# Respacing the weight-sum steps, giving the last weights' narrowing a buffer of its own, and turning block 0's rows inside the last expert tile

## The chip, the cores and the metric

The kernel runs on one core of a Trainium2 chip. What counts is the device time of one launch in microseconds (us), as the median of several runs. Five engines work side by side, each through a queue of its own that it takes in order: TensorE (PE, matmuls), VectorE (DVE), ScalarE (ACT), GpSimd (POOL) and SyncE (SP, which only issues transfers). ACT and POOL issue transfers too, in line with their other work.

## What is computed

Three stages over 4608 rows of 512 numbers:

```python
x = attention(q, k, v)                      # chunks of 64, 8 heads
# mixture of experts: rows with x @ w_skip > 0 go to the best of 8 experts
h = np.maximum(xc[mask] @ w1[e], 0.0)       # 512 -> 1024
y[mask] = gate_w[mask, None] * (h @ w2[e])  # 1024 -> 512
out[do_compute] = xc + y
# last stage, over all rows ("moe2")
h = np.maximum(np.maximum(x @ w1, x @ w2), x @ w3)   # 512 -> 768
return (h @ w_out).astype(np.float32)                # 768 -> 512
```

The four weight matrices of the last stage come in 64-bit floats and are narrowed to 32 bits on the chip.

## The kernel before

Every product is made of three matmuls: each operand is split into a high part that TensorE takes exactly and the rest, and high*high, low*high and high*low are added (`mm3`, L705 to L707). The high part is an ACT cast (L90, L517, L575, L884), the low part a subtraction on DVE or POOL (L91, L518, L576, L885).

Attention takes the first 213 us. Then the experts run one after the other, e = 0 to 7. `first_tiles` makes h for the expert's first row tiles in four pieces, called h_0, h_2, h_4 and h_6 here (hhi on ACT L711, hlo on DVE L712), and then y by `second`; after y, DVE adds it to the rows (xg<-y, L694) and POOL scatters them to x_dram (L696). A third tile (`single`) and more of them stand behind branches on the expert's row count (L983, L916, L920). When such a branch is not taken, all engines meet there, and TensorE goes on with the next expert only after DVE has passed the branch too. In this input experts 1, 4 and 6 end at the first such branch; expert 0's always runs its third tile, and experts 2, 3 and 5 take the branch.

The last stage turns x by a 2x2 block scheme with seven products in place of eight. Its weights therefore have to be narrowed, added up and split in advance: 18 steps, two for each of nine units (matrix m = 0 to 2, column block f = 0 to 2). A step is `sums_ahead(i)`: load n_raw, narrow it into n_q (DVE L531, L532, L533, L536 and an ACT square L534), four sums on DVE (L569 to L572), the ACT cast L575, the DVE remainder L576, and two stores to m2_sums: the high part from the ACT queue (L577), the low part from SP, or for i >= 11 from POOL (L578). Steps 0 to 10 run among the experts: the table STEPS says how many in each, and `first_tiles` puts one behind a piece of h. In the experts n_q is one buffer, so a step's first instruction waits for the store of the step before it. Steps 11 to 17 run in block 0 of the last stage, one in each of units 0 to 6; there n_raw has three buffers (shared with raw_m, below) and n_q two, of the tag "s4".

The last stage goes over five blocks of rows. For a block `sums_T` turns the rows (PE trf L879, tr11, tr12, tr21, tr22), makes the sums t1 to t4 (DVE L893 to L900) and splits everything. Each of the nine `unit`s then makes seven products into three accumulators a, b and d. An accumulator is used again after another engine has read it: ACT copies the first a (p1), the first d (p5) and the second a (u2), DVE adds the third a to p5 (L1034) before the fourth goes into the same place. The weights of a product (ws) come back from m2_sums by SP loads through a ring (L851). At the end of a block come the products with w_out (o). The six halves of w_out are narrowed by `m2_direct` in block 0: load raw_m (POOL queue, L812), narrow into n_q_m, split into whi_m and wlo_m. A scheduler writes the order of each engine's queue; the program gives it dependencies and a few lower bounds (`issue_after`).

In the names of the traced rows the numbers are left out: n_q stands for n_q0 to n_q17, f_a for the accumulator a of any unit.

## Time and profile before

| | us |
|---|---|
| median of 3 runs | 1106.93 (1106.44 to 1108.24) |
| the profiled execution | 1109.83, span 1108.1 |
| PE busy | 1042.2 (94%) |
| DVE busy | 614.8 (55%) |
| ACT busy | 446.2 (40%) |
| POOL busy | 309.1 (28%) |

The profile is of one execution. PE is busy nearly all of it; the granted clock of TensorE is at its full level but for short stretches at half. What a change can give is therefore in the places where PE waits, and in the stretches at half clock. A row of a timeline gives the start and the length of an instruction, its engine, its line and what it writes and reads, and in brackets how long the engine had idled before it and what ended that.

### The profile page before, as it was taken

To read this page: it belongs to the slowest core of one execution; us is meant where nothing else is said; L and a number is where in the kernel's file an instruction comes from. 1 tells how busy PE (TensorE), PEld (TensorE's weight loads), DVE (VectorE), ACT (ScalarE), POOL (GpSimd) and SP (SyncE) were. 2 spreads that over 40 slices of the span, in tenths; PEclk is the share of its full clock that TensorE was granted. 3 is DMA by queue.
4 is the path that set the end of the run, shared out by engine and by line. 5 is a ranking of instruction groups with operands and counts; after the bars stand their busy time and mean duration, and the time that the engine had idled before them with its cause. 6 is when DMAs were issued, how large, how long until landed. Compare 5 with 4: busy or idle time off the path is not lost.

```text
span 1108.1 us, 17499 instructions
## 1 busy us (share of the span) xinstructions
PE 1042.2 (94%) x6320; PEld 872.1 (79%) x6320; DVE 614.8 (55%) x1299; ACT 446.2 (40%) x774; POOL 309.1 (28%) x297
## 2 busy tenths in 40 slices
PE   7899799988899998998899799999999999999997
PEld 6788677777788787887687588878888888788996
DVE  6687588756756477671499772335244442443241
ACT  6677487434434244431444342222322232223231
POOL 4124232364404044320432160222312140123021
PEclk9999799999899999999999999999999999999999
DMA  9999996257764468544898934663566545666591
GB/s 211 195 216 232 261 229 183 89 195 259 265 217 136 138 211 273 192 150 141 274 319 285 300 114 136 197 190 114 165 194 192 166 139 166 183 186 208 186 288 38
DMA packets 217513, 216.99 MB, mean 196 GB/s; under 512 B 50219, under 2 KB 179403, under 8 KB 217408
## 3 DMA queue, kind: packets, MB, share of 16 engines
q1 hardware_dynamic: 206384, 183.62, 57.3%
q0 software_dynamic: 8432, 23.76, 6.6%
q10 hardware_dynamic: 2592, 8.26, 1.9%
q8 instruction: 60, 0.98, 0.4%
q14 instruction: 45, 0.37, 0.1%
HBM read 175.15 MB, written 41.83 MB: 196 GB/s over the span
## 4 chain that ended last, share of the span: by engine, by line
PE 41%; DMA 6%; DVE 3%; issue 3%; POOL 1%; ACT 0%; SPq 0%; POOLq 0%; DVEq 0%; ACTq 0%
PE f_a L705 5%; PE f_a L707 5%; PE f_a L706 5%; PE o L705 4%; PE o L707 4%; PE o L706 4%; DMA ws<-m_sums 3%; PE f_d L705 3%; PE f_d L707 3%; PE f_d L706 3%; DMA m_sums<-n_q 2%; PE f_b L705 1%; PE f_b L707 1%; PE f_b L706 1%; PE trf L879 1%
## 5 line engine op out<-in xcount | busy, mean ns | idle before, releaser
L91 POOL TENSOR_TENSOR fh<-best,fh 128x512 fp32r<-128x512 f32 (+1 forms) x60 | 77.0, 1290 | 356.3 <-ACT fh L90 270.4
L705 PE MATMUL f_a<-x_t,ws 128*128 128x512 f32 (+1 forms) x270 | 100.7, 373 | 5.0 <-DVE p L1034 4.8
L706 PE MATMUL f_a<-x_t,ws 128*128 128x512 f32 (+1 forms) x270 | 99.9, 370 | 0.0
L707 PE MATMUL f_a<-x_t,ws 128*128 128x512 f32 (+1 forms) x270 | 99.7, 370 | 0.0
L90 ACT CAST whi_e<-raw_e 128x1024 fp32r<-128x1024 f32 x64 | 65.1, 1045 | 60.0 <-DMA raw_e<-in_moe_w_dram 34.8
L705 PE MATMUL h<-xhi,whi_e 128*128 128x256 f32 x256 | 75.5, 295 | 12.2 <-DVEq L983 7.0
L706 PE MATMUL o<-wlo_m,fh 128*128 128x512 f32 x216 | 84.6, 392 | 0.0
L705 PE MATMUL o<-whi_m,fh 128*128 128x512 f32 x216 | 83.4, 392 | 0.0
L707 PE MATMUL o<-whi_m,fh 128*128 128x512 f32 x216 | 83.4, 392 | 0.0
L91 DVE TENSOR_TENSOR wlo_e<-raw_e,whi_e 128x1024 fp32r<-128x1024 f32 x50 | 67.1, 1351 | 18.1 <-ACT whi_e L90 15.9
L705 PE MATMUL y<-whi_e,hhi 128*128 128x512 f32 x184 | 74.3, 406 | 2.6 <-ACT hhi L772 1.8
L707 PE MATMUL y<-whi_e,hlo 128*128 128x512 f32 x184 | 72.8, 400 | 1.8 <-DVE hlo L712 1.6
L706 PE MATMUL h<-xlo,whi_e 128*128 128x256 f32 x256 | 74.4, 291 | 0.0
L707 PE MATMUL h<-xhi,wlo_e 128*128 128x256 f32 x256 | 74.3, 290 | 0.0
L706 PE MATMUL y<-wlo_e,hhi 128*128 128x512 f32 x184 | 72.3, 395 | 0.0
L696 POOL DMA_INDIRECT x_dram<-xg,ids_sb x20 | 20.6, 1030 | 180.2 <-DVE xg L694 72.8
L90 ACT CAST fh<-best 128x512 fp32r<-128x512 f32 (+1 forms) x60 | 34.7, 579 | 89.5 <-DVE best L1036 57.9
L1039 ACT COPY p<-f_a 128x512 f32<-128x512 f32 (+1 forms) x45 | 24.5, 545 | 99.3 <-PE f_a L707 99.1
L705 PEld LDWEIGHTS h<-xhi,whi_e 128*128 128x128 f32 x256 | 51.0, 199 | 15.3 <-ACTq L983 6.3
L705 PEld LDWEIGHTS f_a<-x_t,ws 128*128 128x128 f32 x270 | 51.2, 190 | 14.5 <-DVE p L1034 5.3
L707 PEld LDWEIGHTS f_a<-x_t,ws 128*128 128x128 f32 x270 | 51.2, 190 | 8.6
L706 PEld LDWEIGHTS f_a<-x_t,ws 128*128 128x128 f32 x270 | 51.2, 190 | 8.3
(226 smaller groups left out, 2678.7 us busy)
## 6 DMA issues: line engine op xcount, KB each, us to landing
ws<-m_sums SPq DMA_DIRECT2D x135, 512.0 KB, 5.2
raw_e<-in_moe_w_dram SPq DMA_DIRECT2D x64, 512.0 KB, 5.1
ws<-m_sums SPq DMA_DIRECT2D x45, 256.0 KB, 3.9
v_bd<-in_v_dram SPq DMA_DIRECT2D x144, 64.0 KB, 4.2
x<-x_dram SPq DMA_DIRECT2D x36, 256.0 KB, 4.9
out_dram<-os SPq DMA_DIRECT2D x36, 256.0 KB, 2.0
x_dram<-xg SPq DMA_DIRECT2D x17, 512.0 KB, 4.2
m_sums<-n_raw ACTq DMA_DIRECT2D x18, 448.0 KB, 6.0
```

What stands on the lines that cost most here:

```text
L90: nc.scalar.copy(hi, src),
L91: eng.tensor_tensor(lo, src, hi.bitcast(F32), op=ALU.subtract),
L696: ins = nc.gpsimd.indirect_dma_start(out=x_dram[:, :], out_offset=bass.IndirectOffsetOnAxis(ap=ids, axis=0), in_=xg, in_offset=None, bound ...
L705: nc.tensor.matmul(acc, ahi, bhi, start=first, stop=False, skip_group_check=onto)
L706: nc.tensor.matmul(acc, ahi, blo, start=False, stop=False, skip_group_check=onto)
L707: return nc.tensor.matmul(acc, alo, bhi, start=False, stop=last, skip_group_check=onto)
L879: nc.tensor.transpose(tr[:, i * P:(i + 1) * P], row[:, c * P:(c + 1) * P], ident)
L1039: nc.scalar.copy(p1, acc_a)
```

## The change

Four edits. (1) STEPS gives expert 0 one step in place of two and expert 5 two in place of one, and the second step of an expert is put behind the piece h_4 in place of h_2. (2) `m2_direct` narrows into a buffer of its own (n_q_m, one of them) in place of the two "s4" buffers that it shared with the steps. (3) The six pieces of w_out come one after unit 3, one after unit 6, two after units 7 and 8; before it was two after each of units 6, 7 and 8. (4) In `sums_T` the split of tr22 comes before the two sums that read it, and block 0's first `sums_T` is issued after the third of eight kf steps of the last expert tile's y, in place of ahead of that y.

```diff
-    def second(name, key, hhi, hlo, i, xg, ids, tag=None):
+    def second(name, key, hhi, hlo, i, xg, ids, tag=None, inside=None):
...
-                mm3(acc, hhi[:, kf, sl], hlo[:, kf, sl], bhi[:, kf % 2, :], blo[:, kf % 2, :], n == 0, n == 7)
+                done = mm3(acc, hhi[:, kf, sl], hlo[:, kf, sl], bhi[:, kf % 2, :], blo[:, kf % 2, :], n == 0, n == 7)
+            if inside and n == 2:
+                with tc.issue_after(done.ins):
+                    inside()
...
-            if n % 2 == 2 - per and side:
+            if n in (0, 4) and side:
...
-    STEPS = [2, 2, 2, 2, 2, 1, 0, 0]
+    STEPS = [1, 2, 2, 2, 2, 2, 0, 0]
...
-        quarters = four_kb([P, 8, P], F32, f"n_q_m{m}_{f}_{half}", True)
+        quarters = fpool.tile([P, 8, P], F32, tag="n_q_m", name=f"n_q_m{m}_{f}_{half}", bufs=1)
...
         tr22 = turned(cc + 2, 1)
+        split_x("b22", tr22, nc.vector)
         nc.vector.tensor_tensor(t2, tr22, t1, op=ALU.subtract)
         nc.vector.tensor_tensor(t3, tr22, b12, op=ALU.subtract)
-        split_x("b22", tr22, nc.vector)
...
-                single(f"{e}_2", (e, 2), *third, lambda: sums_T(0, 0))
+                single(f"{e}_2", (e, 2), *third, inside=lambda: sums_T(0, 0))
...
+        SPREAD = [0, 0, 0, 1, 0, 0, 1, 2, 2]
...
-                if b == 0 and 3 * f + m >= 6:
-                    for _ in range(min(2, len(rest))):
-                        rest.pop(0)()
+                for _ in range(SPREAD[3 * f + m] if b == 0 else 0):
+                    rest.pop(0)()
```

The number of instructions on each engine stays the same. Their order does not, and three places follow. Lines behind the edits stand three or four lower (L694 stays, L983 becomes L986, L1034 becomes L1037).

The first place is DVE at the end of expert 1. n_q1 and n_q2 are the buffers of its two steps, y_1_0 and y_1_1 its two row tiles. Before:

```order
L576 TENSOR_TENSOR n_q1_3965<-n_q1_3965,n_raw1_3963 128x896
L712 SCALAR_TENSOR_TENSOR hlo_1_4542<-h_1_4_4629,hhi_1_4541 128x512
L91 TENSOR_TENSOR wlo_e2_3_4532<-raw_e2_3_4529,whi_e2_3_4531 128x1024
L712 SCALAR_TENSOR_TENSOR hlo_1_4542<-h_1_6_4656,hhi_1_4541 128x512
...
L531 TENSOR_SCALAR n_q2_4572<-n_raw2_4570 128x512
...
L694 SCALAR_TENSOR_TENSOR xg_1_3854<-y_1_0_4714,xg_1_3854 128x512
...
L576 TENSOR_TENSOR n_q2_4572<-n_q2_4572,n_raw2_4570 128x896
L694 SCALAR_TENSOR_TENSOR xg_1_3854<-y_1_1_4743,xg_1_3854 128x512
L973 TENSOR_LOAD cnt_i_130 x2
L983 COMPARE_AND_BRANCH
```

Now:

```order
L91 TENSOR_TENSOR wlo_e2_3_4516<-raw_e2_3_4513,whi_e2_3_4515 128x1024
L712 SCALAR_TENSOR_TENSOR hlo_1_4526<-h_1_6_4640,hhi_1_4525 128x512
L576 TENSOR_TENSOR n_q1_4556<-n_q1_4556,n_raw1_4554 128x896
...
L531 TENSOR_SCALAR n_q2_4626<-n_raw2_4624 128x512
L532 SCALAR_TENSOR_TENSOR n_q2_4626<-n_raw2_4624,n_q2_4626 128x512
L694 SCALAR_TENSOR_TENSOR xg_1_3854<-y_1_0_4698,xg_1_3854 128x512
...
L694 SCALAR_TENSOR_TENSOR xg_1_3854<-y_1_1_4727,xg_1_3854 128x512
L576 TENSOR_TENSOR n_q2_4626<-n_q2_4626,n_raw2_4624 128x896
L976 TENSOR_LOAD cnt_i_130 x2
L986 COMPARE_AND_BRANCH
```

The first step's end (L576 of n_q1, and with it its store) moved behind the piece h_6; the second step's first instruction stayed where it was, ahead of both xg<-y and of the branch.

The second place is ACT in block 0, around unit (m=1, f=1). f_0_2_1_a is accumulator a of the next unit in block 0, p1_0_2_1 its copy; n_q_m3_0_0 is the first half of w_out. Before:

```order
L534 ACTIVATE n_q15_8745<-n_raw15_8664 128x512
L1054 COPY best_0_0_1_2_8655<-f_0_0_1_a_8647 128x512
L575 CAST n_raw14_8566<-n_q14_8666 128x896
L577 DMA m2_sums_1_2_167<-n_raw14_8566 128x896
L1039 COPY p1_0_2_1_8815<-f_0_2_1_a_8812 128x512
L1043 COPY p5_0_2_1_8817<-f_0_2_1_d_8814 128x512
```

Now:

```order
L575 CAST n_raw14_8566<-n_q14_8666 128x896
L534 ACTIVATE n_q_m3_0_0_8726<-raw_m3_0_0_8724 128x512
L1057 COPY best_0_0_1_2_8655<-f_0_0_1_a_8647 128x512
L577 DMA m2_sums_1_2_167<-n_raw14_8566 128x896
L534 ACTIVATE n_q16_8839<-n_raw16_8755 128x512
L90 CAST whi_m3_0_8722<-n_q_m3_0_0_8726 128x512
L575 CAST n_raw15_8664<-n_q15_8757 128x896
L577 DMA m2_sums_1_2_167<-n_raw15_8664 128x896
L575 CAST n_raw16_8755<-n_q16_8839 128x896
L1042 COPY p1_0_2_1_8827<-f_0_2_1_a_8824 128x512
```

The square of n_q_m3_0_0 now stands ahead of the store of step 14, and the square and the cast of step 16 ahead of the copy p1 of unit (2, 1). On POOL the loads of the same stretch were, before:

```order
L547 DMA n_raw15_8664<-in_moe2_w2_dram 128x2x512
L578 DMA m2_sums_0_2_166<-n_q13_8568 128x896
L91 TENSOR_TENSOR fh_0_0_0_8636<-best_0_0_0_2_8396,fh_0_0_0_8636 128x512
L547 DMA n_raw16_8743<-in_moe2_w3_dram 128x2x512
L578 DMA m2_sums_1_2_167<-n_q14_8666 128x896
L547 DMA n_raw17_8825<-in_moe2_w3_dram 128x2x512
```

Now:

```order
L547 DMA n_raw15_8664<-in_moe2_w2_dram 128x2x512
L91 TENSOR_TENSOR fh_0_0_0_8636<-best_0_0_0_2_8396,fh_0_0_0_8636 128x512
L578 DMA m2_sums_0_2_166<-n_q13_8568 128x896
L815 DMA raw_m3_0_0_8724<-in_moe2_w_out_dram 128x1024
L578 DMA m2_sums_1_2_167<-n_q14_8666 128x896
L547 DMA n_raw16_8755<-in_moe2_w3_dram 128x2x512
```

The load of raw_m3_0_0 took the place of the load of n_raw16, which went into the place of n_raw17's; the two after step 13 and after step 14 each wait for that step's high store, which frees their buffer.

The third place is DVE in the same unit; u2_0_1_1 and p5_0_1_1 are read out of accumulators d and a of unit (1, 1). Before:

```order
L1034 TENSOR_TENSOR u2_0_1_1_8734<-u2_0_1_1_8734,f_0_1_1_d_8732 128x512
L572 TENSOR_TENSOR n_q14_8666<-n_q14_8666 128x128
L531 TENSOR_SCALAR n_q15_8745<-n_raw15_8664 128x512
L1036 TENSOR_TENSOR best_0_0_1_1_8654<-best_0_0_1_1_8654,u2_0_1_1_8734 128x512
L532 SCALAR_TENSOR_TENSOR n_q15_8745<-n_raw15_8664,n_q15_8745 128x512
L1034 TENSOR_TENSOR p5_0_1_1_8735<-p5_0_1_1_8735,f_0_1_1_a_8730 128x512
```

Now:

```order
L1037 TENSOR_TENSOR u2_0_1_1_8746<-u2_0_1_1_8746,f_0_1_1_d_8744 128x512
L532 SCALAR_TENSOR_TENSOR n_q15_8757<-n_raw15_8664,n_q15_8757 128x512
L531 TENSOR_SCALAR n_q_m3_0_0_8726<-raw_m3_0_0_8724 128x512
L1039 TENSOR_TENSOR best_0_0_1_1_8654<-best_0_0_1_1_8654,u2_0_1_1_8746 128x512
L576 TENSOR_TENSOR n_q14_8666<-n_q14_8666,n_raw14_8566 128x896
L533 SCALAR_TENSOR_TENSOR n_q15_8757<-n_raw15_8664,n_q15_8757 128x512
L532 SCALAR_TENSOR_TENSOR n_q_m3_0_0_8726<-raw_m3_0_0_8724,n_q_m3_0_0_8726 128x512
L1037 TENSOR_TENSOR p5_0_1_1_8747<-p5_0_1_1_8747,f_0_1_1_a_8742 128x512
```

Between the two reads stand six rows where four stood, and the first instruction on raw_m3_0_0 is among them. On PE the fourth product into f_0_1_1_a now follows the third at once; before, four other products lay between.

## Rows read from the trace of the kernel before

**Rows 1.** What PE waited for: engine, line, releaser; us in total, times, longest.

```profile
PE h L705 <- DVEq L983: 7.0, 3, 3.8
PE f_a L705 <- DVE p L1034: 4.8, 1, 4.8
PE f_a L705 <- DMA ws<-m_sums: 2.3, 2, 1.8
```

**Rows 2.** Busy time by stretch: bounds, length, engines (instructions), granted clock, DMA share, GB/s.

```profile
261.30:274.56 13.26, 13.26 (x98) 13.26 (x99) 13.01 (x16) 8.40 (x10) 9.03 (x5) 0.87 0.75 254
290.59:305.00 14.41, 14.41 (x98) 14.41 (x99) 11.98 (x12) 7.96 (x10) 9.79 (x6) 0.79 0.83 275
343.94:355.69 11.75, 11.75 (x98) 11.75 (x99) 10.22 (x16) 8.32 (x11) 7.78 (x7) 1.00 0.71 231
519.78:530.09 10.31, 8.92 (x39) 7.16 (x38) 2.06 (x3) 1.48 (x3) 0.00 (x0) 0.83 1.07 343
554.00:609.40 55.40, 54.88 (x244) 44.92 (x243) 51.66 (x93) 23.92 (x38) 15.52 (x18) 1.00 0.91 302
609.40:637.10 27.70, 21.06 (x86) 16.23 (x85) 21.82 (x36) 10.20 (x18) 5.46 (x8) 0.94 0.90 300
```

**Rows 3.** Timeline at the ends of experts 0 and 1.

```profile
260.15 0.43 DVE L531 TENSOR_SCALAR n_q<-n_raw 128x512 int32<-128x512 int32 x1 [5.35 <-DMA m_sums<-n_q]
261.30 0.39 PE L705 MATMUL h<-xhi,whi_e 128*128 128x256 f32 x1 [2.81 <-ACTq L916]
274.41 0.46 SPq L578 DMA_DIRECT2D m_sums<-n_q  x1
277.98 0.68 DVE L712 SCALAR_TENSOR_TENSOR hlo<-h,hhi 128x512 fp32r<-128x512 f32 x1
283.19 0.43 DVE L531 TENSOR_SCALAR n_q<-n_raw 128x512 int32<-128x512 int32 x1 [1.61 <-DMA m_sums<-n_q]
290.59 0.55 PE L705 MATMUL h<-xhi,whi_e 128*128 128x256 f32 x1 [3.78 <-DVEq L983]
```

**Rows 4.** Timeline from the end of expert 4 into expert 5.

```profile
408.52 1.75 SPq L97 DMA_DIRECT2D raw_e<-in_moe_w_dram  x3
420.27 0.36 PE L705 MATMUL h<-xhi,whi_e 128*128 128x256 f32 x1 [1.73 <-DVEq L983]
426.34 0.43 DVE L531 TENSOR_SCALAR n_q<-n_raw 128x512 int32<-128x512 int32 x1 [6.28 <-DMA m_sums<-n_q]
438.78 0.50 PE L707 MATMUL y<-whi_e,hlo 128*128 128x512 f32 x1 [1.64 <-DVE hlo L712]
```

**Rows 5.** Timeline, PE's waits at the start of block 0.

```profile
521.90 0.41 PE L879 MATMUL trf<-ident,x 128*128 128x128 f32 x1 [1.39 <-DMA x<-x_dram]
534.35 0.41 PE L879 MATMUL trf<-ident,x 128*128 128x128 f32 x2 [2.16 <-DVE x_b L885]
546.13 0.33 PE L879 MATMUL trf<-ident,x 128*128 128x128 f32 x1 [1.16 <-DMA x<-x_dram]
```

**Rows 6.** Timeline in block 0, units (1, 1) and (2, 1): POOL, ACT and DVE.

```profile
584.65 0.73 POOL L547 DMA_DIRECT2D n_raw<-in_moe_w_dram  x1 [2.73 <-DMA m_sums<-n_raw]
585.52 0.68 DVE L1034 TENSOR_TENSOR u<-u,f_d 128x512 f32<-128x512 f32 x1
587.07 0.94 ACT L575 CAST n_raw<-n_q 128x896 fp32r<-128x896 f32 x1
587.86 0.68 DVE L1034 TENSOR_TENSOR p<-p,f_a 128x512 f32<-128x512 f32 x1
588.04 0.33 ACTq L577 DMA_DIRECT2D m_sums<-n_raw  x1
595.84 0.71 POOL L547 DMA_DIRECT2D n_raw<-in_moe_w_dram  x1 [5.42 <-DMA m_sums<-n_raw]
```

**Rows 7.** DMA issues between 560 and 620 us: count, KB each, median us to landing.

```profile
n_raw<-in_moe_w_dram POOLq DMA_DIRECT2D x4, 512.0 KB, 5.5
raw_m<-in_moe_w_out_dram POOLq DMA_DIRECT2D x4, 512.0 KB, 4.7
```

More of the change, by code (lines that the diff above doesn't have):

```diff
@@ L750, in first_tiles, with single @@
         return hhi, hlo
-    def single(name, key, xT, xg, ids, between=None):
+    def single(name, key, xT, xg, ids, between=None, inside=None):
         e = key[0]
@@ L774, in single @@
         nxt = between() if between else None
-        second(name, key, hhi, hlo, 0, xg, ids)
+        second(name, key, hhi, hlo, 0, xg, ids, inside=inside)
         return nxt
@@ L1059 @@
         rest = [lambda i=i, half=half: m2_direct(3, i, wpool2, half) for i in range(NS) for half in range(2)]
+        SPREAD = [0, 0, 0, 1, 0, 0, 1, 2, 2]
     else:
         rest = [lambda i=i: m2_piece(3, i, wpool2) for i in range(NS)]
+        SPREAD = [0, 0, 0, 0, 0, 0, 1, 1, 1]
     steps = list(range(AHEAD, 2 * len(UNITS)))
```

## The prediction

> **What bounds the kernel now.** I read the page first: PE is busy 94% of the span, so only PE's waits and its stretches at half clock can be won or lost. The list of PE's waits [rows 1] names three sorts that the change touches: the branches at the ends of experts (7.0 us in three waits), one wait of 4.8 for a DVE read of an accumulator, and two for the weights ws. The table by stretch [rows 2] then shows what a wait does to the clock. The 98 matmuls of an expert's h take 11.75 us at full clock; behind the waits at the ends of experts 0 and 1 they take 13.26 and 14.41, with a granted clock of 0.87 and 0.79, that is, with part of the stretch at 1.2 GHz instead of 2.4. In block 0 the row from 554 to 609 us is the important one: PE has next to no gap, 0.227 us per matmul (55.40 over 244), 1.36 us per product of six, 9.5 us per unit, but DVE is busy 51.66 of 55.40. It has some 0.6 us to spare in each unit. The next row (609 to 637) is where PE loses: 21.06 busy of 27.70. Last come the timelines around each wait [rows 3 to 6] and the landing times [rows 7].
>
> **The change, part by part.** Times are on the clock of the profiled execution.
>
> End of expert 0. DVE's L531 of a second step stood 5.35 us for the last store, and xg<-y and the branch behind it; PE waited 2.81 [rows 3]. That step is gone there. What is late next is the branch itself: at the end of expert 4, where DVE is on time, PE waits 1.73 [rows 4], and at full clock afterwards. So 1.1 of the wait and 13.26 - 11.75 = 1.5 of clock: -2.6 (bounds -3 and -1).
>
> End of expert 1. The second step's L531 has kept its place ahead of both xg<-y and the branch, but the store it waits for has moved back: L576 of the first step now stands behind hlo of h_6, which ended at 278.66, and ends an estimated 1.1 later (0.68 for 512 columns, 896 here), at 279.8, where it was issued at 274.41 [rows 3]. That store needed 8.8 us (274.41 to 283.19), since it stood behind loads; the quickest transfers of this size in the rows take 4.7, the usual 5.5 [rows 7]. So L531 starts between 284.5 and 288.6, and I take 5.5: 285.3, 2.1 later than before. From L531 to PE's first matmul it was 7.4 us of the same instructions: PE starts 2.1 later. +2.1 (bounds -1, as L531 idled 1.61, and +5.4); the clock stays as bad as it was.
>
> End of expert 4. This one had no step in its way. Now a whole second step stands between wlo_e and the branch, xg<-y inside it, and its L531 waits for the first step's store, which SP issues only behind the raw_e loads from 408.52 to 410.27 [rows 4]. At 5.5 to 8.8 us it lands between 415.8 and 419.1; 7.4 later PE would start at 423.2 to 426.5, against 420.27. If the store is early, only the cast and L576 behind the last xg<-y are left, about 1. I take +3.5, toward the 8.8 because the store stands behind loads in both places, and 1.5 of clock, as after the 2.81: +5.0 (bounds +0.5 and +7.7).
>
> Expert 5. Its first L531 was the first thing on DVE and idled 6.28 with all wlo_e and hlo behind it, and PE waited 1.64 for a late hlo [rows 4]. It now stands behind hlo of h_0, so the idle time is covered by those: -1.6, and 1.5 of clock, -3.1 (bounds -3.5 and 0). The step that moves into expert 5 meets a branch that is taken, where PE doesn't wait: 0.
>
> Start of block 0. Nine matmuls of y (0.25 each, 2.2 us) now stand ahead of the first transposes, which waited 1.39 for x [rows 5]; the stretch ran at 0.83 [rows 2], so 3.5 of its 10.31 us at half clock, 1.7 lost. Both go. The 2.16 for x_b shrinks to about 0.5: the bank's last reader is one DVE instruction (0.68) earlier, and six matmuls (1.4) stand ahead of the transpose. The 1.16 for block 1's rows goes, since 30 matmuls were put ahead. -1.4 - 1.7 - 1.7 - 1.2 = -6.0; I take -5.5 for a wait on the sums' casts that may take their place (bounds -7 and -3).
>
> Units of block 0. What is removed: 4.8 and 2.3 of waits [rows 1] and 0.06 of 27.70 for the clock [rows 2], 1.7: 8.8. What is put there hangs on three transfers in a row. The load of raw_m_0_0 takes n_raw16's place, 584.65 [rows 6]; it waits for step 13's store as that did. It lands 4.7 later [rows 7], 589.3. Its L531 on DVE comes two instructions after the read of u, at 586.7, and waits 2.6. Behind it stand L1039, L576, L533, L532 and the read p5 of accumulator a: by 0.68 (0.43 for L531, 1.1 for L576), with the ends overlapped by 0.08, 4.0 us; p5 ends at 593.3. PE's fourth product into that accumulator used to have four products of cover; now it follows the third at once, and the third was done by 587.86, when DVE read it. PE waits 5.5.
>
> On ACT the store of step 14 stands behind the square of that same raw_m and a copy: 590.6 instead of 588.04. n_raw16's load waits for it. In the rows this took 7.8 (588.04 to 595.84); with the 5.5 of rows 7 in mind I take 6.3: 596.9. The load takes 5.5: 602.4. DVE goes from there to the last sum of step 16 in 5.4 (seven of 0.6, L576, four sums at 0.2), ACT casts for 0.94, and only then comes the copy p1 that PE's second product in unit (2, 1) needs: 609.4. PE has four products until there, 593.3 + 5.4 = 598.7. It waits 10.7. A third wait, in place of the 4.8, is a bare read of an accumulator with nothing between: 1.2. With 1.5 of clock behind the long one: 5.5 + 10.7 + 1.2 + 1.5 = 18.9, less 8.8: +10. Bounds: if no transfer is late, the first wait is 2.9, the second 0, and it is 4.1 - 8.8 = -4.7; if all three take 7.8, 8.6 + 14.6 + 2.7 - 8.8 = +17.
>
> The Trainium skill ("DMA: Bandwidth & Descriptors", section "Anatomy of one DMA — SWDGE (gpsimd) path") gives a transfer as 2.0 us and its bytes at 436 GB/s, an estimate of 3.2 us for 512 KB. By that the chain would be short: the units come to about +2 and both expert ends to about 0, a total of -9. Rows 7 have 4.7 and 5.5 for these loads with other traffic beside them, so I don't go by it. The same page ("Issuing engines are not separate DMA queues") has transfers of all issuing engines share the same 16 engines; with a DMA share of 0.91 in rows 2 that speaks against bringing a piece of w_out forward, and would add the 1.7 us that 512 KB take at that row's 302 GB/s.
>
> End of block 0. Four groups of transposes follow each other where o matmuls lay between; casts of 0.6 to 0.7 separate their banks: +0.5 (0 to 2). The one buffer of n_q_m makes the narrowings serial; each is some 3 us on DVE and the o products that need the last come over 7 us after unit 8: 0.
>
> Sum: -2.6 + 2.1 + 5.0 - 3.1 - 5.5 + 10 + 0.5 = +6.4. The profiled execution is 1109.83, span 1108.1 and 1.7 around it; it lies 2.9 above the median, and I carry the difference over: 1113.3.
>
> **The rivals.** First, the other side: DVE and ACT reach the moved rows after their data have landed. Then all old waits go and little comes: -2.6, -1.0, +0.5, -3.1, -5.5, -4.7, +0.5, -15.9 in all, 1091. For it: the waits named in rows 1 all lie where the edits are. Against it: in rows 6 a load that stands behind a store was issued 7.8 after it. It decides at landing times: with transfers at 3.2 the total is the -9 above, 1098. These two: 0.24.
>
> Second, the long wait is halved, because step 14 and raw_m come some 5 us sooner against PE, and expert 4's end costs 1: units +5, -2.6 + 2.1 + 1 - 3.1 - 5.5 + 5 + 0.5 = -2.6, 1104 to 1108. Rows 2 give DVE 3.7 us of slack over 5.8 units, which could carry half of that. 0.20.
>
> Third, all of it late at 7.8: the units +17, experts 1 and 4 +5.4 and +7.7, 19.4 in all, 1126. Rows 7 have most transfers quicker. 0.06.
>
> **How the numbers follow.** The forecast, 1113, has 0.50, and 1107 to 1120 as its own range. Runs of the kernel before lie within 1.8 us of each other, so 0.2% (2.2 us) is about what can be told from no change. Faster by more: the first rival, and the lower half of the second, 0.33. Within: 0.15, the rest of the second and the edge of the forecast. Slower: 0.52. For 8 in 10 the range goes from 1095 to 1121.
>
> **What would show it.** In the profile after: PE's wait at the end of expert 0 at 1.5 to 1.8 with h at 11.75; at the ends of experts 1 and 4 waits of 5 to 6 for DVE's branch; no wait for x at the start of block 0. In block 0 the copy p1 behind the casts L575 as PE's longest wait, 10 us, one of 5 for DVE's p in the unit ahead of it, and POOL's n_raw load idle for m_sums<-n_raw. I am wrong if DVE and ACT don't idle at raw_m and n_raw16, and if PE's waits between 585 and 637 come to less than 9 us.

## The result, and the profile after

The kernel after takes 1120.6 us (median of 4 runs, 1119.13 to 1125.96) against 1106.68 for the kernel before (4 runs). The ratio is 1.0133, 95% interval 1.0098 to 1.0169. It is slower, as forecast, and by 13.9 us where 6.4 were forecast: the sign was right, and so were most places, but the forecast was less than half of what came. A second comparison (e11 below) gave 1.0119 (1.0071 to 1.0168). The profiled execution of the kernel after took 1120.28, span 1118.6; that of the kernel before was 1109.83.

The list of PE's waits in the kernel after, from 230 to 670 us (engine, line, what was waited for; us in total, times, longest), against [rows 1]:

```profile
PE h L705 <- ACTq L986: 14.9, 2, 8.6
PE f_a L705 <- DVE p L1037: 7.5, 2, 6.7
PE f_a L705 <- ACT p L1042: 6.1, 1, 6.1
PE h L705 <- DVEq L986: 1.8, 1, 1.8
PE f_a L705 <- DMA ws<-m_sums: 0.9, 1, 0.9
```

The waits at the first branch of an expert (L983 before, L986 now) have gone from 3.8 at most to 8.6 and 6.3. In block 0 there are now two long waits, 6.7 for DVE's p and 6.1 for ACT's p, where one of 4.8 stood. The waits for x at the start of block 0 are not in the list any more.

Busy time by stretch of the kernel after (bounds, length, then PE, PEld, DVE, ACT and POOL with their instructions, granted clock, DMA share, GB/s), against [rows 2]:

```profile
259.48:271.20 11.72, 11.72 (x98) 11.72 (x99) 10.94 (x9) 7.70 (x10) 9.48 (x5) 1.00 0.88 272
289.75:303.20 13.45, 13.45 (x96) 13.45 (x97) 10.23 (x9) 8.12 (x10) 9.00 (x6) 0.84 0.84 300
426.20:440.20 14.00, 14.00 (x101) 14.00 (x102) 11.71 (x11) 8.32 (x11) 9.82 (x6) 0.85 0.94 313
579.79:636.99 57.20, 43.49 (x167) 34.22 (x166) 43.69 (x77) 19.53 (x32) 12.78 (x18) 0.85 0.78 260
587.50:597.80 10.30, 5.68 (x13) 4.46 (x14) 7.57 (x15) 1.70 (x3) 1.99 (x3) 0.50 0.79 258
604.60:611.40 6.80, 4.81 (x11) 3.80 (x12) 2.83 (x5) 3.02 (x5) 1.75 (x3) 0.50 0.93 309
```

Behind expert 0 the h of the next expert now runs at full clock (98 matmuls in 11.72, 13.26 before). Behind the ends of experts 1 and 4 it runs at 0.84 and 0.85. In block 0 PE is busy 43.49 of 57.20, and two pieces of it are at half clock: 5.68 and 4.81 us of matmuls at 1.2 GHz, which would take about half of that at 2.4, so by estimate 5.2 us are lost to the clock there.

How long the stages last, in two profiled executions of each kernel (before and e1; after and e11, all below). A stage ends where the next expert's first matmul of h starts, or at the matmul named, counted among those into the accumulators of the units (378 of them are block 0's). The row of expert 0 starts 15.0 us after that expert's first matmul of h, in all four alike, and the last row ends with PE's last matmul:

| stage | before | e1 | after | e11 | change of the means | forecast |
|---|---|---|---|---|---|---|
| expert 0 | 33.10 | 30.30 | 30.43 | 32.36 | -0.3 | -1.1 |
| expert 1 | 29.29 | 27.01 | 30.27 | 29.59 | +1.8 | +0.6 |
| expert 2 | 53.35 | 50.83 | 52.56 | 52.16 | +0.3 | 0 |
| expert 3 | 50.16 | 50.21 | 51.29 | 52.05 | +1.5 | 0 |
| expert 4 | 26.18 | 27.29 | 32.60 | 32.17 | +5.7 | +3.5 |
| expert 5 | 42.46 | 39.37 | 39.71 | 39.74 | -1.2 | -1.6 |
| expert 6 | 25.44 | 25.38 | 25.77 | 25.81 | +0.4 | 0 |
| expert 7 to the 181st matmul | 93.29 | 90.96 | 88.11 | 88.50 | -3.8 | -5.5 |
| 181st to 391st matmul | 92.14 | 94.38 | 103.52 | 104.21 | +10.6 | +10.5 |
| the rest | 427.94 | 429.43 | 428.72 | 430.25 | +0.8 | 0 |
| sum | 873.35 | 865.16 | 882.98 | 886.85 | +15.7 | +6.4 |

The forecast's terms are put where they act: the slow clock behind a wait belongs to the stage after it. Attention comes ahead of these stages and is not in the table. It took 213 to 216 us in some of the profiled executions and 221 to 228 in others, the kernel before and the kernel after among both, so times are compared within one table row or one ratio only.

### The profile page after: what moved, and what is told of

Its sections match the earlier page's. It is cut to its first block, busy times and chain, and to the rows that moved or that the text cites. A ratio compares the mean times of both kernels' runs of the same rounds, so it can differ in the third digit from the quotient of the medians.

```text
span 1118.6 us, 17488 instructions
## 1 busy us (share of the span) xinstructions
PE 1044.0 (93%) x6320; PEld 873.2 (78%) x6320; DVE 609.2 (54%) x1299; ACT 447.5 (40%) x774; POOL 313.1 (28%) x297
## 4 chain that ended last, share of the span: by engine, by line
PE 44%; DMA 6%; issue 1%; DVE 1%; ACT 1%; POOL 1%; SPq 0%; ACTq 0%; POOLq 0%; DVEq 0%
PE f_a L705 6%; PE f_a L706 6%; PE f_a L707 6%; PE o L705 4%; PE o L706 4%; PE o L707 4%; DMA ws<-m_sums 4%; PE f_d L705 3%; PE f_d L706 3%; PE f_d L707 3%; PE f_b L706 1%; PE f_b L707 1%; PE f_b L705 1%; PE trf L882 1%; DMA m_sums<-n_raw 1%
## 5 line engine op out<-in xcount | busy, mean ns | idle before, releaser
L705 PE MATMUL f_a<-x_t,ws 128*128 128x512 f32 (+1 forms) x270 | 101.4, 376 | 13.6 <-DVE p L1037 7.5
L705 PE MATMUL h<-xhi,whi_e 128*128 128x256 f32 x256 | 75.5, 295 | 19.6 <-ACTq L986 14.9
L696 POOL DMA_INDIRECT x_dram<-xg,ids_sb x20 | 23.2, 1162 | 182.5 <-DVE xg L694 92.2
L1042 ACT COPY p<-f_a 128x512 f32<-128x512 f32 (+1 forms) x45 | 24.4, 544 | 91.3 <-PE f_a L707 91.0
```

The lines of the kernel that those rows point to most:

```text
L696: ins = nc.gpsimd.indirect_dma_start(out=x_dram[:, :], out_offset=bass.IndirectOffsetOnAxis(ap=ids, axis=0), in_=xg, in_offset=None, bound ...
L705: nc.tensor.matmul(acc, ahi, bhi, start=first, stop=False, skip_group_check=onto)
L1042: nc.scalar.copy(p1, acc_a)
```

## The experiments

**e1, the kernel before once more.** No edit.

> The kernel before, unchanged, profiled once more. Theory A (the 2.9 us by which its profiled execution lay above its median belong to that one execution): the new profiled execution lies at 1105.5 to 1108.5, and one or two stretches account for the difference. Rival B (a profiled execution is longer than others by about 3 us whatever the kernel): it lies at 1109 to 1111 again. The kernel after speaks against B already, since its profiled execution (1120.28) lies at its median (1120.6).

Ratio 0.9991 (0.9963 to 1.0020), so two equal kernels compare equal to about 0.3% here. The profiled execution lay at 1109.47, the lowest of ten (median 1117.37). That is in the range that B named, but by luck: B has a profiled execution longer than the others, and this one was shorter, so B falls. A's level was missed too, since all runs of that comparison were some 10 us longer. Its second half holds: the wait at the end of expert 0 was 1.51 where it was 2.81 in [rows 3], and expert 5's wait for a late hlo [rows 4] was not there at all; the two stages were 2.8 and 3.1 shorter, and expert 1 by 2.3.

**e2, edit 4 alone.**

```diff
...
         tr22 = turned(cc + 2, 1)
+        split_x("b22", tr22, nc.vector)
         nc.vector.tensor_tensor(t2, tr22, t1, op=ALU.subtract)
         nc.vector.tensor_tensor(t3, tr22, b12, op=ALU.subtract)
-        split_x("b22", tr22, nc.vector)
...
-                single(f"{e}_2", (e, 2), *third, lambda: sums_T(0, 0))
+                single(f"{e}_2", (e, 2), *third, inside=lambda: sums_T(0, 0))
```

> The kernel before with edit 4 alone (split of tr22 ahead of the two sums, block 0's first transposes inside the last y). Theory A (each edit pays at its own place): -5 to -6 at the start of block 0 and nothing in the experts, 1101 to 1102; the waits in units 5 to 8 of block 0 (7 us before) stay within 2. Rival B (the scheduler lays the units out anew once the start moves, so that the loss of units 4 to 6 is partly edit 4's): a new wait of 3 us or more between 575 and 615 us, and 1104 or more.

Ratio 0.9951 (0.9914 to 0.9988): -5.5 us, as A has it. Expert 7 to the 181st matmul took 86.11, against 93.29, 90.96, 89.96 (e4) and 90.84 (e5) in the kernels that have neither edit 4 nor the new STEPS. PE's waits in e2 from 500 to 675 us:

```profile
PE f_a L705 <- DVE p L1037: 5.1, 1, 5.1
PE h L705 <- DVEq L992: 1.6, 1, 1.6
PE f_b L705 <- DMA ws<-m_sums: 0.8, 1, 0.8
```

The waits for x and x_b of [rows 5] are gone, and nothing new stands between 575 and 615. One part of A is wrong: the wait of 5 for DVE's p in unit 7 stayed (4.8 before, 5.1 here).

**e3, edit 1 alone; e5, only the place of the second step; e6, only the table.**

```diff
# e5 has this line alone, e6 the table alone, e3 both
-            if n % 2 == 2 - per and side:
+            if n in (0, 4) and side:
...
-    STEPS = [2, 2, 2, 2, 2, 1, 0, 0]
+    STEPS = [1, 2, 2, 2, 2, 2, 0, 0]
```

> The kernel before with edit 1 alone (STEPS and the place of the second step). Theory A: -2 at the end of expert 0, +6 at the end of expert 4 with a wait of 8 to 9 us at the branch, -3 in expert 5, together +1 to +3: 1108 to 1110. Rival B (the wait of 8.63 at the end of expert 4 was a slow store of that execution): a wait of 5 us there, as forecast, and -2 to 0 in all: 1105 to 1107.

> The kernel before with the second step of an expert behind h_4 in place of h_2, and STEPS as it was. Theory A (the place makes the loss of edit 1: the second step's narrowing starts a store's time too late for an expert that ends at its first branch): waits of 5 us or more for the branch at the ends of experts 1 and 4, each with slow clock behind it; +6 to +9 us, a ratio of 1.005 to 1.008. Rival B (the table makes it, through the step that came into expert 5): waits of 4 us or less at both, ratio 0.998 to 1.002.

> The kernel before with the new STEPS and the second step behind h_2 as it was. Theory A: end of expert 4 as in the kernel before (wait 1.7 to 2.7), expert 5 no longer than in the other kernels, since its branch is taken: ratio 0.997 to 1.000. Rival B: the second step in expert 5 costs 2 us or more there or at expert 6: ratio 1.003 or more.

e3: 1.0073 (1.0037 to 1.0109), 8.2 us, more than either theory gave it; the long wait at the end of expert 4 that A named is there (8.35). e5: 0.9983 (0.9956 to 1.0010), nothing. e6: 1.0075 (1.0040 to 1.0111). So A was wrong in e5 and in e6: the place costs nothing and the table costs all. B of e6 has the ratio but not the place: expert 5 took 39.81 and expert 6 25.82, as in the stage table, and the loss stands at the end of expert 4. PE's first matmul behind the end of expert 4, in e5 and then in e6 (start, length, engine, line, in brackets the wait):

```profile
432.47 0.36 PE L705 MATMUL h<-xhi,whi_e 128*128 128x256 f32 x1 [1.80 <-DVEq L983]
```

```profile
436.20 0.58 PE L705 MATMUL h<-xhi,whi_e 128*128 128x256 f32 x1 [8.62 <-ACTq L983]
```

The order of DVE's queue says why. The steps are a chain through the one buffer n_q: none can start before the store of the last has landed. With two steps in expert 0, step 6 starts ahead of expert 3's branch (369.20 in the kernel before), step 7 in expert 4's h (404.31), and step 8 behind expert 4's branch (426.34). With one step in expert 0 steps 5 to 7 come 14 to 25 us later, counted from the first matmul of h: step 6 starts with expert 4's h (395.38 in the kernel after), step 7 between the last hlo and the branch (419.10). The place h_4 or h_2 is only a lower bound, and in e5 it moved none of the three to another side of a branch.

**e4, edits 2 and 3 alone.**

```diff
-        quarters = four_kb([P, 8, P], F32, f"n_q_m{m}_{f}_{half}", True)
+        quarters = fpool.tile([P, 8, P], F32, tag="n_q_m", name=f"n_q_m{m}_{f}_{half}", bufs=1)
...
+        SPREAD = [0, 0, 0, 1, 0, 0, 1, 2, 2]
...
```

> The kernel before with edits 2 and 3 alone (own buffer for n_q_m, pieces of w_out after units 3, 6, 7, 8). Theory A (the first piece in unit 3 makes the loss): waits of 5 us or more for DVE's p in unit (1, 1) and for ACT's copy p1 of unit (2, 1), 13 us or more of waits and slow clock beyond the 8.8 that go, +8 to +12: 1115 to 1119. Rival B (the loss needs the order that all four edits make together): less than +4, up to 1111, without the wait for the copy p1.

Ratio 1.0045 (1.0012 to 1.0079), 5.0 us: between the two. PE's waits in e4 from 580 to 690 us:

```profile
PE f_a L705 <- DVE p L1034: 6.8, 1, 6.8
PE f_a L705 <- ACT p L1039: 2.5, 1, 2.5
PE f_a L705 <- DMA ws<-m_sums: 1.7, 1, 1.7
```

Both waits of A are there, the second at 2.5 where the kernel after has 6.1. In e4's order ACT's cast and store of step 14 stand ahead of the square of step 15, which waited 2.96 for the low store of step 13; in the kernel after they stand behind it. Counted from the 181st matmul (583.02 in e4, 579.79 in the kernel after) the store was issued at 3.1 against 8.4, and step 16, whose n_raw waits for it, began on DVE at 16.2 against 19.6. From the 181st to the 391st matmul e4 took 99.89, 6.7 more than the mean 93.2 of six executions without the own buffer and with two pieces after each of units 6, 7 and 8 (before, e1, e2, e3, e5, e6; 91.7 to 95.3, and e9, which is also of this kind, 91.2); the kernel after took 103.9.

The ratios of e2, e3 and e4 multiply to 1.0069, 7.7 us, where all four edits together cost 13.9 and, in e11, 13.3. So by their middle values the edits cost more together than one by one, though the intervals are wide enough to hide it. Of the difference 4.0 can be placed: the units took 103.9 with all edits and 99.89 in e4, with the second wait at 6.1 in place of 2.5. The rest is not placed.

**e7, the kernel after without the piece in unit 3.**

```diff
-        SPREAD = [0, 0, 0, 1, 0, 0, 1, 2, 2]
+        SPREAD = [0, 0, 0, 0, 0, 0, 2, 2, 2]
```

> The kernel after with SPREAD = [0, 0, 0, 0, 0, 0, 2, 2, 2]: own buffer for n_q_m, but no piece of w_out after unit 3. Theory A (that piece makes the loss of the units): no wait of PE above 3 us between 575 and 615 us, the stretch from unit 3 to block 1 as in the kernel before or up to 3 longer (11.4 longer in the kernel after); edit 1's +6 to +8 and edit 4's -5 remain: ratio 1.000 to 1.004. Rival B (one buffer for n_q_m makes the loss, wherever the pieces stand): waits for DVE's p or for ws behind unit 6 take it over, 6 us or more longer than before: ratio 1.007 or more.

Ratio 1.0056 (1.0020 to 1.0093). PE's waits in e7 from 595 to 695 us:

```profile
PE f_a L705 <- DVE p L1037: 2.5, 1, 2.5
PE f_a L705 <- DMA ws<-m_sums: 2.5, 1, 2.5
PE trf L882 <- DVE t L900: 1.0, 1, 1.0
```

No wait above 3, and none of the two long ones: A, though the ratio lies between the two theories. The 181st to the 391st matmul took 95.9, 2.7 more than the mean of 93.2: A's "up to 3". So of the 10.7 by which the kernel after is above that mean, some 8 are the piece after unit 3. The other 2.7 go with the own buffer, but one execution stands against six that spread from 91.7 to 95.3, so that size is rough. The piece after unit 3 in the shared buffers was not run.

**e12, edits 4 and 2, the pieces as before.** e2 with the own buffer of e4.

> The kernel before with edits 4 and 2 (own buffer for n_q_m), the pieces two after each of units 6, 7 and 8 as before. Theory A (the own buffer by itself takes away the wait for step 17's store): 4.8 us and 1.7 of slow clock go in unit 7, against which the one buffer adds no more than 3: ratio 0.990 to 0.994. Rival B (a second piece in the one buffer waits for the split of the first, and DVE stands behind it): a wait of 2 to 5 us for DVE's p or for ws in units 7 and 8 as in the kernel after without the piece in unit 3, ratio 0.995 to 1.000.

Ratio 0.9978 (0.9958 to 0.9998), B. The wait for p fell from 5.1 to 2.6, and a wait of 2.9 for ws and of 1.0 for a transpose came up; the 181st to the 391st matmul took 95.58, against 91.73 in e2. In both places where it was tried without the early piece the units were longer with the own buffer, by 2.7 and 3.9, each from one execution.

**e8, the kernel after with the own buffer for raw_m in place of n_q_m.**

```diff
-        raw = rpool.tile([P, 1024], I32, tag="raw", name=f"raw_m{m}_{f}_{half}")
+        raw = fpool.tile([P, 1024], I32, tag="raw_m", name=f"raw_m{m}_{f}_{half}", bufs=1)
...
-        quarters = fpool.tile([P, 8, P], F32, tag="n_q_m", name=f"n_q_m{m}_{f}_{half}", bufs=1)
+        quarters = four_kb([P, 8, P], F32, f"n_q_m{m}_{f}_{half}", True)
```

> The kernel after with the own buffer given to raw_m in place of n_q_m (n_q_m in the two s4 buffers again), pieces after units 3, 6, 7, 8 as in the kernel after. No load of n_raw waits for a store that stands behind raw_m's narrowing any more, and raw_m's first load waits for no step. Theory A (the chain of transfers makes the loss, as the prediction has it): neither the wait of 6.7 for p5 nor that of 6.1 for the copy p1; the stretch from unit 3 to block 1 no more than 3 longer than before: ratio 1.000 to 1.004. Rival B (the amount of work that the piece puts on DVE in units 4 and 5 makes it, 6 instructions between two reads of accumulators): a wait of 3 us or more for DVE's p stays in unit (1, 1), ratio 1.006 or more.

Ratio 1.0129 (1.0058 to 1.0200). PE's waits in e8 from 590 to 700 us:

```profile
PE f_a L705 <- DMA ws<-m_sums: 3.7, 1, 3.7
PE o L705 <- ACT whi_m L90: 2.5, 1, 2.5
PE trf L882 <- ACT t L893: 2.2, 1, 2.2
PE f_a L705 <- ACT u L1048: 1.9, 2, 1.6
PE f_a L705 <- DVE p L1037: 1.7, 1, 1.7
```

A's mechanism holds: neither long wait is there. A's size does not: 103.5 from the 181st to the 391st matmul, no better than the kernel after. The scheduler brought block 1's first transposes forward into the units (the trf wait at 622.16). A piece of w_out could be loaded only when the one before it had left the one buffer of raw_m: DVE idled 0.67, 1.52 and 3.55 for the last three loads, and the o products waited for whi_m. The time came back elsewhere, and B's ratio came without B's wait.

**e9, edit 4 and a table that leaves the ends of experts 1, 4 and 6 free.**

```diff
-    STEPS = [2, 2, 2, 2, 2, 1, 0, 0]
+    STEPS = [1, 1, 2, 2, 0, 2, 1, 2]
```

> The kernel before with edit 4 and STEPS = [1, 1, 2, 2, 0, 2, 1, 2], second step behind h_2 as before. In this table no step's first instruction stands between the last hlo and the branch at the ends of experts 1, 4 and 6; one (step 10) does at the end of expert 7. Theory A (such an instruction, held by the store of the step before, is what each expert's end waits for): end of expert 1 down from 3 to 4.5 us to about 1.7 with its slow clock gone (-2 to -4), expert 4 as in the kernel before (1.7 to 2.7), and the wait moves to the end of expert 7, 4 to 8 us there in place of 1.6. Rival B (the ends are set by the number of steps before them, through the loads): expert 4's end keeps 5 us or more, and expert 7's stays at 1.6.

Ratio 0.9945 (0.9911 to 0.9978), the same as edit 4 alone. The waits of PE around the ends of experts 1 and 4 in e9:

```profile
299.45 0.36 PE L705 MATMUL h<-xhi,whi_e 128*128 128x256 f32 x1 [2.92 <-PEq L986]
...
425.04 0.80 PE L705 MATMUL y<-whi_e,hhi 128*128 128x512 f32 x1 [2.62 <-ACT hhi L711]
434.98 0.35 PE L705 MATMUL h<-xhi,whi_e 128*128 128x256 f32 x1 [1.97 <-PEq L986]
```

The end of expert 4 is at 1.97, which speaks for A, and the end of expert 1 at 2.92, above the 1.7 that A gave it and within the 1.84 to 4.98 of the old table. At the end of expert 7 it was 2.44, not 4 to 8. But a wait of 2.62 for hhi inside expert 4, one of 2.31 in expert 3 and stages of experts 3 and 4 that were 4.2 and 4.3 longer than in the first profile of the kernel before took the gain back.

**e10, edit 4 and later pieces.**

```diff
-                if b == 0 and 3 * f + m >= 6:
-                    for _ in range(min(2, len(rest))):
-                        rest.pop(0)()
+                for _ in range([0, 0, 0, 0, 0, 0, 1, 2, 3][3 * f + m] if b == 0 else 0):
+                    rest.pop(0)()
```

> The kernel before with edit 4 and the pieces of w_out one after unit 6, two after unit 7, three after unit 8, narrowed in the s4 buffers as before. Theory A (the wait of 4.8 us for DVE's p in unit 7 is a narrowing that waits for step 17's store, and a piece that comes a unit later finds it landed): that wait falls under 1.5, and the end of block 0 gets no longer by more than 1: ratio 0.990 to 0.994. Rival B (DVE is too full before the o products, whatever the order): 3 us or more of waits for wlo_m, whi_m or the sums at the end of block 0, ratio 0.995 to 1.000, as with edit 4 alone.

Ratio 0.9923 (0.9890 to 0.9956), the fastest of all, though its interval and e2's overlap. A is wrong about the wait. In the timeline of e10:

```profile
619.67 0.75 POOL L578 DMA_DIRECT2D m_sums<-n_q  x1 [0.33 <-DVE n_q L576]
...
625.85 0.43 DVE L531 TENSOR_SCALAR n_q_m<-raw_m 128x512 int32<-128x512 int32 x1 [2.22 <-DMA m_sums<-n_q]
627.40 0.68 DVE L1037 TENSOR_TENSOR p<-p,f_a 128x512 f32<-128x512 f32 x1
628.13 0.79 PE L705 MATMUL f_a<-x_t,ws 128*128 128x512 f32 x1 [5.31 <-DVE p L1037]
```

The second piece's L531 still stands ahead of the read p and still waits for step 17's store; the end of block 0 got no longer, so B's waits did not come either. The ratio lies in A's range without A's reason, so it is no support for A. From the 181st to the 391st matmul e10 took 91.43 and e2 91.73: that the later pieces gain anything over edit 4 alone is not shown.

**e11, the kernel after once more.** No edit.

> The kernel after, unchanged, against the kernel before on one chip. Theory A (its loss is the sum over places of edit 1, +8 at expert 4, 3 and 1, of edits 2 and 3, +7 to +10 in units 4 to 8, and of edit 4, -4): ratio 1.010 to 1.014, waits of 8 to 10 at the end of expert 4, 6 to 7 for p5 in unit (1, 1) and 5 to 7 for p1 in unit (2, 1). Rival B (part of the 13.9 us belongs to the chip and to single executions): ratio under 1.008, with one of these waits gone.

Ratio 1.0119 (1.0071 to 1.0168), and every wait of A at its place: 8.21 at the end of expert 4, 6.59 for p5, 5.26 for p1. The loss belongs to the kernel.

**e13 and e14, who sets the end of expert 4.** In the kernel after, DVE's remainder of step 6 takes 5.56 us where others take 1.09, beside two POOL instructions:

```profile
404.95 4.74 POOL L91 TENSOR_TENSOR wlo_e<-raw_e,whi_e 128x1024 fp32r<-128x1024 f32 x2
405.08 5.56 DVE L576 TENSOR_TENSOR n_q<-n_q,n_raw 128x896 fp32r<-128x896 f32 x1 [1.06 <-ACT n_raw L575]
...
410.67 0.36 SPq L578 DMA_DIRECT2D m_sums<-n_q  x1
...
419.10 0.43 DVE L531 TENSOR_SCALAR n_q<-n_raw 128x512 int32<-128x512 int32 x1 [2.98 <-DMA m_sums<-n_q]
...
426.20 0.58 PE L705 MATMUL h<-xhi,whi_e 128*128 128x256 f32 x1 [8.63 <-ACTq L986]
```

In the kernel before the same two POOL instructions (405.18 to 409.90) held DVE in expert 4 as well, at L532 of step 7:

```profile
404.31 0.43 DVE L531 TENSOR_SCALAR n_q<-n_raw 128x512 int32<-128x512 int32 x1
404.77 5.68 DVE L532 SCALAR_TENSOR_TENSOR n_q<-n_raw,n_q 128x512 int32<-128x512 int32 x1
```

```diff
# e13
-        nc.vector.tensor_tensor(seven.bitcast(F32R), seven, hi.bitcast(F32), op=ALU.subtract)
+        (nc.gpsimd if i == 6 else nc.vector).tensor_tensor(seven.bitcast(F32R), seven, hi.bitcast(F32), op=ALU.subtract)
# e14, on the kernel after
-                    expert_piece(e + 1, i, free.pop(0), nc.gpsimd if i in (0, 1) else None, raw)
+                    expert_piece(e + 1, i, free.pop(0), nc.gpsimd if i in (0, 1) and e != 4 else None, raw)
```

> The kernel after with the remainder L576 of step 6 (the step whose end lies in expert 4) on POOL, behind POOL's two splits of wlo_e, in place of DVE. On DVE it took 5.56 us there in place of 1.09, from 405.08 to 410.64, since POOL's two splits ran until 409.69. Theory A (the store of that step, which starts when the remainder is done and lands 8.4 later, sets the end of expert 4): the remainder ends about 1 to 2 us later than before on POOL, so the wait at the branch becomes 9 to 11 us, though DVE is not held. Rival B (what DVE had to do behind the held remainder, the last hlo and the wlo_e splits, sets it): the wait falls to 5 to 6 us.

> The kernel after with the two splits of wlo_e that POOL makes during expert 4 on DVE, so that nothing of POOL runs beside the remainder of step 6. The order moves with it: step 6 ends behind hlo of h_6, its store stands two loads later on SP, step 7 starts between the two xg<-y. Theory A (the held remainder, through its store, makes the wait of 8.6; a store 8 us before the branch is what counts): the remainder takes 1.1 us but ends no earlier, the store is issued at or after the same point of the expert, and the wait at the branch stays at 7 us or more. Rival B (the hold itself is the price, worth its 4.5 us): the wait falls to 3 to 5 us.

e13, one run (1119.79; the kernel before 1109.13 beside it):

```profile
410.23 2.12 POOL L576 TENSOR_TENSOR n_q<-n_q,n_raw 128x896 fp32r<-128x896 f32 x1
...
412.38 0.33 SPq L578 DMA_DIRECT2D m_sums<-n_q  x1
...
419.34 0.43 DVE L531 TENSOR_SCALAR n_q<-n_raw 128x512 int32<-128x512 int32 x1 [2.54 <-DMA m_sums<-n_q]
...
426.45 0.58 PE L705 MATMUL h<-xhi,whi_e 128*128 128x256 f32 x1 [8.25 <-ACTq L986]
```

The wait stays at 8.25, so B falls: DVE was not held, and it waited for the store all the same. A's number fails too. Counted from expert 4's first matmul (393.60, in e13 394.24) the store was issued 1.1 later and landed 0.4 sooner, after 7.0 us in place of 8.4. e14, one run (1116.61):

```profile
417.01 0.43 DVE L531 TENSOR_SCALAR n_q<-n_raw 128x512 int32<-128x512 int32 x1
...
421.06 0.69 DVE L533 SCALAR_TENSOR_TENSOR n_q<-n_raw,n_q 128x512 int32<-128x512 int32 x1
...
421.85 0.36 PE L705 MATMUL h<-xhi,whi_e 128*128 128x256 f32 x1 [2.32 <-DVE n_q L533]
```

The remainder takes 1.09, from 412.55, and the store goes out at 413.67, later than in the kernel after; yet the wait falls to 2.32, under both theories. Step 7 starts on DVE at 417.01, between the two xg<-y, and all but its first two instructions stand behind the branch. Counted from expert 4's first matmul (394.55) its L531 came at 22.5 in place of 25.5, and PE went on 4.8 after it in place of 7.1: 3.0 of the gain is the store's earlier landing, 2.3 that most of the step no longer stands ahead of the branch. Expert 6's end has 5.04 instead of 1.78: there the whole of step 10, which started 7.3 later against its expert than in the kernel after, stands ahead of the branch, as it does in the kernel after. So the held remainder is not the price, as e13 shows by itself; a step that starts late ahead of a branch is.

Of the versions run, edit 4 alone (0.9951), with the table of e9 (0.9945) and with the pieces of w_out later (0.9923) were the fastest; their intervals overlap, and the whole gain is under 1%.

## Why the prediction was right and where it failed

What PE waited at the ends of the experts, over the profiled executions of seven kernels with the old STEPS (before, e1, e2, e4, e5, e10, e12) and of seven with the new ones (after, e3, e6, e7, e8, e11, e13; e14 is left out, since it changes the order in expert 4):

| wait | old, mean | range | new, mean | range | change | forecast |
|---|---|---|---|---|---|---|
| end of expert 0 | 2.20 | 0.62 to 3.33 | 1.06 | 0.40 to 2.98 | -1.1 | -1.1 |
| end of expert 1 | 3.56 | 1.84 to 4.98 | 5.85 | 4.17 to 7.06 | +2.3 | +2.1 |
| end of expert 4 | 1.97 | 1.73 to 2.72 | 8.54 | 7.92 to 9.79 | +6.6 | +3.5 |
| late hlo in expert 5 | 1.14 | 0 to 2.29 | 0 | | -1.1 | -1.6 |

*Ends of experts 0 and 1.* Right, in mechanism and in the change of the wait, though at the end of expert 0 both levels lay lower than told (2.20 and 1.06 for 2.81 and 1.73). The clock was not: of "1.5 of clock" behind expert 0 the stages show less, since in three of the seven old kernels h ran at full clock there, so that nothing was to be won.

*End of expert 4.* This is the largest step that failed: "I take +3.5, toward the 8.8 because the store stands behind loads in both places". The mechanism was as told, a whole step between wlo_e and the branch and its L531 held by the store, and the size was not: +6.6 was measured. By the prediction's own figures a landing after 5.5 gives +2.9 and one after 8.8 gives +6.2, so +3.5 lies at the early end and not toward the 8.8. The store landed at 419.1, the late end of the 415.8 to 419.1 that the prediction gave, and from L531 to PE it was 7.1 of the forecast 7.4. The bound, +7.7 with the clock, was right; the value taken inside it was not. There are three more things here that the prediction did not see. "This one had no step in its way" is not so: in the kernel before step 7 ran from 404.31 to 419.41, all of it ahead of the same branch; its L531 waited for nothing, and PE's wait was 1.73. The same shift makes expert 3 1.5 longer, for which there was no term (51.59 in e6, which has the new table alone, and 50.25 in e5, which has the old one). And DVE's remainder is held by POOL, which turned out to cost nothing (e13).

*Expert 5.* The stall of 1.64 in [rows 4] stood in four of the seven old kernels (1.64, 2.00, 2.29 and 2.08) and in three it did not. The term of -3.1 was read from an execution that had it, so the -1.2 in the stage table is what it is worth on the mean.

*Start of block 0.* Right in place: the waits for x went, 0.5 to 0.9 for ws came. Worth -3.8 in the table and -5.5 by e2's ratio, for -5.5 forecast.

*Units of block 0.* +10 and +0.5 (with the end of block 0) were forecast and 10.6 came. That the sums agree is luck, since the parts differ:

| part | forecast | after |
|---|---|---|
| wait for p5 | 5.5 | 6.7 |
| wait for the copy p1 | 10.7 | 6.1 |
| bare read | 1.2 | 0.8 |
| slow clock | 1.5 | 5.2 |
| sum | 18.9 | 18.8 |

The timeline of the kernel after, against [rows 6]:

```profile
579.80 0.57 POOL L578 DMA_DIRECT2D m_sums<-n_q  x1
...
583.40 0.55 POOL L815 DMA_DIRECT2D raw_m<-in_moe_w_out_dram  x1 [3.02 <-DMA m_sums<-n_raw]
586.49 0.43 DVE L531 TENSOR_SCALAR n_q<-n_raw 128x512 int32<-128x512 int32 x1 [4.10 <-DMA m_sums<-n_q]
588.17 0.33 ACTq L577 DMA_DIRECT2D m_sums<-n_raw  x1
588.24 0.42 DVE L531 TENSOR_SCALAR n_q_m<-raw_m 128x512 int32<-128x512 int32 x1
...
591.38 0.68 DVE L1037 TENSOR_TENSOR p<-p,f_a 128x512 f32<-128x512 f32 x1
592.12 0.80 PE L705 MATMUL f_a<-x_t,ws 128*128 128x512 f32 x1 [6.72 <-DVE p L1037]
593.76 1.43 POOL L547 DMA_DIRECT2D n_raw<-in_moe_w_dram  x2 [2.65 <-DMA m_sums<-n_raw]
599.39 0.43 DVE L531 TENSOR_SCALAR n_q<-n_raw 128x512 int32<-128x512 int32 x1 [4.31 <-DMA n_raw<-in_moe_w_dram]
...
605.96 0.58 ACT L1042 COPY p<-f_a 128x512 f32<-128x512 f32 x1
606.59 0.80 PE L705 MATMUL f_a<-x_t,ws 128*128 128x512 f32 x1 [6.10 <-ACT p L1042]
```

The first wait had another cause than the one told. The step that failed is "Its L531 on DVE comes two instructions after the read of u, at 586.7, and waits 2.6". DVE did not idle at raw_m: it came there at 588.24, with no wait. It had idled 4.10 ahead of that, at L531 of step 15, for the low store of step 13, which POOL issued at 579.80. In the order of before that L531 stands behind the read of u; now it stands ahead of it and of the read p5. The front part showed it: before, L531 of step 15 is a row between the two reads, and now its L532 is the first row behind u, so that L531 has moved ahead. The prediction did not follow it up. Nor did it follow POOL: the split of fh now stands ahead of that low store, which went out 1.46 later against the 181st matmul than in the kernel before (579.80 against 579.79, 580.01 against 581.46). In e4, where the order is another, DVE idled 2.54 at raw_m and 1.24 at step 15, with 6.8 for PE: there the forecast cause is seen too.

The second wait is the chain as told but for its first link. The high store of step 14 was to be late behind raw_m's square, which was to wait for raw_m; the square did not wait (588.04). The store was issued at 588.17, as soon as its cast was done, and the cast had stood on ACT behind the square of step 15, which waited 4.57 for the same low store of step 13. Against the 181st matmul the store was 1.8 later than in the kernel before (8.4 and 6.6). The larger part is the place that n_raw16's load lost to raw_m, as told: n_raw16's load came 5.6 after the store (6.3 forecast), its L531 5.6 after that (5.5), PE's product behind the copy p1 7.2 after that (7.0). The units ran 1.7 ahead of the kernel before there (181st matmul at 579.79, 581.46 before); on that kernel's clock the wait ended at 608.3, for 609.4 forecast, and began at 602.2, for 598.7, since the first wait ended 0.5 later and the four products between took 8.4 in place of 5.4, largely at half clock. That makes the 4.6 by which it was shorter; 3.7 more than forecast went to the clock. Of the two signs of being wrong that the prediction named, DVE idled at n_raw16 (4.31) but not at raw_m, and PE's three waits there come to 13.6, not to less than 9.

*The sum.* By the stage table the misses are: expert 4 +2.2, block 0's start +1.7, expert 3 +1.5, expert 1 +1.2, expert 0 +0.8, the later blocks +0.8, three of 0.3 to 0.4, the units +0.1; 9.3 together (the two sums differ by 15.7 - 6.4), all of one sign. That is hardly chance. What the change takes away was measured in one execution, 2.9 above its median, in which the waits in question were longer than on the mean: 2.81 against 2.20 at the end of expert 0, 1.64 against 1.14 in expert 5, 93.29 against 91.3 for expert 7 to the 181st matmul (before, e1, e4, e5). The step "it lies 2.9 above the median, and I carry the difference over" takes it that these waits stand in the median at that size. That can account for the misses in experts 0 and 5 and at the start of block 0, 2.9 of the 9.3. Expert 4's 2.2 is the size above, and expert 3's 1.5 had no term. The third rival, all transfers late, gave 1126 and was put at 0.06; the end of expert 4 went its way (+7.7 there), the end of expert 1 (+5.4 there) and the units did not.

*POOL and DVE.* The 5.56 us is no accident: in the seven kernels with the old STEPS one remainder took 5.3 to 5.5, in expert 3, and in six with the new ones 5.5 to 5.6, in expert 4. In all thirteen POOL's two splits ran beside it, and it ended 0.96 after them. The Trainium skill ("SBUF — State Buffer", section "Who interferes with whom") says that a DVE instruction with two SBUF inputs contends with a GpSimd instruction that reads SBUF, and that the second one waits in full; the trace agrees, with two POOL instructions in a row in place of one. It does not agree on which waits: L532 of the kernel before started 0.41 ahead of POOL's first split and was held 5.68 all the same. The hold as such is not new in expert 4, since DVE is held there in the old kernels too, only at another instruction.

*Left open.* Why the store ahead of expert 4's end lands at 419.1 to 419.3 whether it is issued at 410.67 or 412.38 was not tried; the raw_e loads ahead of it on SP are the likely reason. The store landed 8.6, 8.2 and 7.1 us after SP was done with the last of these (after, e13, e14), while counted from its own issue it took 8.4, 7.0 and 3.3; that fits, but the loads were not moved by themselves, so it is argued and not shown. A version of the units with both chains cut, e8's buffer without block 1's transposes moving forward, was not run.

## What to carry to other kernels

A wait that a change takes away is worth its mean over several executions, and a wait that it puts in behind a transfer can come at the late end of its bounds, as at the end of expert 4 here; to take the one from a single long execution and the other from the early end errs in one direction. Where work is chained through one buffer, its phase against the branches can matter more than its issue point: here, moving one step out of expert 0 cost nothing there and 6.6 us four experts on, and moving the issue point cost nothing (e5). A piece of work brought forward must be followed with every instruction whose place it takes, on each queue: here the first long wait began at a neighbour, step 15, that had moved two rows ahead and waited for a store, and the second at a load that had lost its place; at the piece itself neither DVE nor ACT waited.

## What was not expected of the hardware

- A DVE subtraction of 128x896 took 5.56 us in place of 1.09 while POOL ran two subtractions on SBUF operands; on POOL itself it took 2.12 (e13).
- The granted clock of TensorE was at half from 587.5 to 597.8 and from 604.6 to 611.4, each time from within a wait of 6 to 7 us to some 5 us past its end. By estimate these waits cost 2.8 and 2.4 us of clock on top of themselves. Longer waits did not cost more clock in order: in [rows 2] it is 1.5 behind the wait of 2.81 and 2.7 behind that of 3.78, and in the kernel after some 1.9 behind 6.29 and behind 8.63 (96 matmuls in 13.45 and 101 in 14.00, by the 11.75 of 98 at full clock).
- A store of 448 KB that was issued 1.1 us later, counted from its expert's start, landed 0.4 sooner (e13).
